# Both MLPs' second layers by seven block products for eight, in passes over K with partial sums in SBUF

## The chip, the cores and the metric

The kernel runs on one core of one Trainium2 chip. The metric is the device time of one execution in microseconds (us). In the views TensorE is PE (its weight loads PEld), VectorE DVE, ScalarE ACT, GpSimd POOL, and SyncE SP, which issues the transfers.

## The reference

Attention with a causal mask over 2 batches, 12 heads, 448 positions and a head width of 64; then two MLPs one after the other on 896 x 768 values, all float32.

```python
def _moe_ref(x, w_gate, w_val, w_out, rms_g):          # 896 x 768, d_ff 1536
    rms = np.sqrt(np.mean(x * x, axis=-1, keepdims=True) + 1e-06)
    xn = x / rms * rms_g
    g = xn @ w_gate
    silu = g * (1.0 / (1.0 + np.exp(-g)))
    val = xn @ w_val
    return (silu * val @ w_out).astype(np.float32)

def _moe2_ref(x, w_in, w_out):                         # d_ff 2048
    h = np.maximum(x @ w_in, 0.0)
    return (h * h @ w_out).astype(np.float32)
```

## The kernel before

Activations lie with the feature along the 128 partitions and the 448 positions of one batch along the free axis; such a tile is called a row here. A layer's output tile is 128 features x 448 positions of one batch, summed over K in tiles of 128.

A float32 product is made of three products in a rounded type (fp32r): each operand is split into a high part (a rounding copy) and a low part (the difference). `parts` splits a row into a slab of high and low part: a cast at line 208 or 210, a subtraction at line 499. `form` does it for three weight tiles into a `ring` buffer: the cast at the same helper's lines, the subtraction at line 608. `product` (line 615) issues the three matmuls of each K tile, 128 x 128 by 128 x 448, into a PSUM bank `m`, at line 623. `weights` loads 128 x 768 of a weight as raw numbers and puts their bits together in two ScalarE steps (lines 571 and 576) and one VectorE step (line 581).

The first layers of both MLPs run through `halves` (line 669): two output tiles and both batches at once, as a 2 x 2 block product over a K of two halves, by seven block products p1 to p7 for eight. It needs sums of weight tiles (`minus`, line 636), four sums of row blocks (`differences`, line 643; the subtraction is at line 652), and adds of PSUM banks and of copies of them (`snap`, line 251 or 694). One such pair is 63 matmuls, where eight block products would be 72. The bank x carries p1, p6, p7 and p4 one on top of the other; after p1, p6 and p7 its running value is taken out before the next product goes on top. The products are issued in the order p1, p2, p6, p5, p7, p4, p3.

The second layers (`layer`, line 857) run directly: for each output tile and both batches, 3 matmuls for each of 12 K tiles (first MLP, w_out as `wo`) or 16 (second MLP, `w2o`, in two passes over K of 10 and 6 tiles; the first pass leaves its sum in a row, the second adds its bank to it at line 940 and stores the output).

Nothing waits in the program's own order. Every step is a task with a due time, the engines that may do it with an estimated duration each, its predecessors and its buffers. `Order.run` takes them one after the other: for each open task the engine is chosen on which it ends first, with COST added for VectorE ("D") and GpSimd ("P"); of the tasks that can start within 0.1 us of the first, that with the earliest due time goes next. GpSimd's steps and those of VectorE marked `port` (inputs in SBUF alone) are planned as excluding each other, one at a time. The result is a fixed order of instructions on each engine. Buffers of a kind are used in turn: a new one waits until the oldest is free. The 24 slabs are two such rings, `sa` (6) and `sb` (18), the rows `fa` (14) and `fb` (18); `sb` and `fb` are there when attention's buffers have been given back.

```python
            first = min(opt, key=lambda c: (c[1], c[2], c[3]))
            c = min((c for c in opt if c[4] == first[4] and c[1] <= first[1] + SLACK), key=lambda c: (c[2], c[3]))
```

## Time and profile before

| | |
|---|---|
| median of 3 runs | 584.4 us (583.57 to 663.83) |
| profiled execution, its own time | 582.35 us |
| its span (first to last instruction) | 580.6 us |
| TensorE busy | 559.5 us (96%), 3155 instructions |
| VectorE, ScalarE, GpSimd busy | 424.4 (73%), 340.9 (59%), 130.4 us (22%) |
| granted TensorE clock, mean | 0.996 |
| HBM read and written | 61.74 and 2.75 MB |

The busy share of an engine is a mean over stages that differ; it is to be read by stage. A wait is put down to the engine and line that released it. A matmul's own duration in the trace overlaps its neighbours', so the pace of TensorE is read from the starts of groups. An operation that may be done by several engines is listed once for each.

### The profile page before, as it was taken

Reading aid. Unit: us, or ns where it says so; the run is one execution under the profiler, and the core shown is the slowest. Engines: PE = TensorE matmul, PEld = TensorE weight load, DVE = VectorE, ACT = ScalarE, POOL = GpSimd, SP = SyncE. Lnnn points to the kernel's source line nnn. Section 1 sums busy time; section 2 is a strip of 40 time slices with the busy share of each in tenths; the row PEclk is TensorE's granted clock in tenths of the full one; section 3 lists DMA queues with packets and bytes.
Section 4 is the critical chain, followed back from the end, with each engine's and each line's share of the span. In section 5 each row is a group of like instructions: output and inputs, shape, how many; then the busy total and the mean of one; then the engine's idle time right before and its main releaser. Section 6 shows DMA issues by size and latency. Waiting matters only on the chain.

```text
span 580.6 us, 8705 instructions
## 1 busy us (share of the span) xinstructions
PE 559.5 (96%) x3155; PEld 495.1 (85%) x3155; DVE 424.4 (73%) x760; ACT 340.9 (59%) x718; POOL 130.4 (22%) x193
## 2 busy tenths in 40 slices
PE   7998998969999999999999999999999999999997
PEld 4766666859899999998999998899999999999996
DVE  4788898768999988998743549999989974336311
ACT  4778887536757676578644446665666665556100
POOL 3555866140022000040000013311213720000000
PEclk9999999989999999999999999999999999999999
DMA  6265421201325333363354211134332345341111
GB/s 174 82 204 151 150 66 77 109 1 58 104 93 183 110 108 110 108 207 119 110 175 145 105 66 56 56 122 144 115 109 91 123 148 179 114 155 64 64 65 63
DMA packets 19499, 65.06 MB, mean 112 GB/s; under 512 B 2048, under 2 KB 8960, under 8 KB 19456
## 3 DMA queue, kind: packets, MB, share of 16 engines
q1 hardware_dynamic: 19456, 64.50, 33.4%
q8 instruction: 25, 0.41, 0.3%
q14 instruction: 18, 0.15, 0.1%
HBM read 61.74 MB, written 2.75 MB: 111 GB/s over the span
## 4 chain that ended last, share of the span: by engine, by line
PE 87%; DVE 7%; POOL 2%; DMA 1%; ACT 1%; issue 1%; SPq 0%; POOLq 0%; DVEq 0%; ACTq 0%
PE m L623 73%; PE t L408 3%; PE o L446 3%; PE s L305 3%; POOL p L392 2%; DVE sb L499 2%; PE s L318 2%; PE s L817 1%; PE o L441 1%; DMA raw<-in_wg 1%; DVE mx L341 1%; DVE fa L548 1%; DMA qk<-in_qk 1%; DVE ring L608 1%; DVE fa L652 0%
## 5 line engine op out<-in xcount | busy, mean ns | idle before, releaser
L623 PE MATMUL m<-sb,ring 128*128 128x448 f32 x1584 | 333.4, 367 | 7.2 <-DVE fa L761 4.9
L623 PEld LDWEIGHTS m<-sb,ring 128*128 128x128 f32 x1584 | 298.4, 189 | 32.3 <-issue 5.2
L623 PE MATMUL m<-sa,ring 128*128 128x448 f32 x630 | 138.1, 365 | 0.9 <-DVE ring L608 0.9
L623 PEld LDWEIGHTS m<-sa,ring 128*128 128x128 f32 x630 | 118.3, 188 | 10.5 <-DVE ring L608 1.3
L210 ACT CAST ring<-w 128x384 fp32r<-128x384 f32 (+1 forms) x111 | 49.6, 471 | 70.0 <-PE m L623 47.4
L608 DVE TENSOR_TENSOR ring<-w,ring 128x384 fp32r<-128x384 f32 (+1 forms) x111 | 57.6, 537 | 40.8 <-ACT ring L210 40.6
L576 ACT ACTIVATE raw<-raw 128x768 uint32<-128x768 uint8 x70 | 62.4, 894 | 12.1 <-DMA raw<-in_wv 8.6
L581 DVE SCALAR_TENSOR_TENSOR w<-w,raw 128x768 uint32<-128x768 uint32 x64 | 53.1, 831 | 20.9 <-ACT w L571 11.2
L208 POOL TENSOR_SCALAR ring<-st 128x384 fp32r<-128x384 f32 x23 | 12.1, 530 | 222.4 <-DVE st L636 124.4
L571 ACT ACTIVATE w<-raw 128x768 f32<-128x768 f32 x64 | 53.6, 850 | 12.7 <-DVE ring L608 9.3
L608 DVE TENSOR_TENSOR ring<-st,ring 128x384 fp32r<-128x384 f32 x65 | 35.7, 573 | 9.0 <-POOL ring L208 5.6
L210 ACT CAST ring<-st 128x384 fp32r<-128x384 f32 x49 | 24.7, 514 | 18.5 <-DVE st L636 14.7
L341 DVE TENSOR_REDUCE mx<-s 128x2 f32<-128x256 f32 (+2 forms) x36 | 24.0, 686 | 12.3 <-PE s L321 6.7
L251 ACT COPY snap<-m 128x448 f32<-128x448 f32 x37 | 19.8, 534 | 19.6 <-PE m L623 19.3
L392 POOL TENSOR_SCALAR p<-p,r 128x128 f32<-128x128 f32 (+1 forms) x48 | 24.0, 518 | 24.9 <-DVE r L382 18.4
L305 PE MATMUL s<-qk 64*128 64x128 f32 (+2 forms) x144 | 26.5, 448 | 2.3 <-ACT p L366 1.1
L392 POOL TENSOR_SCALAR p2t<-p2t,r 128x256 f32<-128x256 f32 (+1 forms) x36 | 21.9, 625 | 11.0 <-DVE r L382 8.4
L366 ACT ACTIVATE p<-s,nb 128x128 f32<-128x128 f32 (+1 forms) x48 | 22.1, 473 | 1.3 <-ACT nb L346 0.4
L446 PE MATMUL o<-pt,vt 128*64 128x320 f32 (+2 forms) x192 | 20.2, 353 | 0.0
L408 PE MATMUL t<-ident,p 128*128 128x128 f32 x96 | 14.2, 283 | 5.8 <-POOL p L392 5.0
L251 ACT COPY fb<-m 128x448 f32<-128x448 f32 x21 | 11.1, 535 | 14.8 <-PE m L623 14.3
L499 DVE TENSOR_TENSOR sb<-fb,sb 128x448 fp32r<-128x448 f32 x29 | 19.6, 710 | 0.0
(125 smaller groups left out, 623.3 us busy)
## 6 DMA issues: line engine op xcount, KB each, us to landing
raw<-in_w2i SPq DMA_DIRECT2D x16, 768.0 KB, 4.2
raw<-in_wg SPq DMA_DIRECT2D x12, 768.0 KB, 4.7
raw<-in_wv SPq DMA_DIRECT2D x12, 768.0 KB, 4.3
raw<-in_wo SPq DMA_DIRECT2D x12, 768.0 KB, 4.6
raw<-in_w2o SPq DMA_DIRECT2D x12, 768.0 KB, 4.4
qk<-in_qk SPq DMA_DIRECT2D x11, 448.0 KB, 3.8
raw<-in_w2o SPq DMA_DIRECT2D x6, 512.0 KB, 3.9
vt<-in_v SPq DMA_DIRECT2D x12, 128.0 KB, 2.8
```

Source lines behind the costliest of these rows:

```text
L210: eng.copy(o, i)
L251: (nc.scalar.copy if e == "A" else nc.vector.tensor_copy)(o, i)
L305: nc.tensor.matmul(s[:, h, o:o + n], z["qk"][BOTH[h], 0, qs], z["qk"][BOTH[h], 1, :n], start=True, stop=False)
L392: E(e).tensor_scalar(t, t, z["r"][:, k:k + 1], 1.0, ALU.mult, ALU.mult)
L408: nc.tensor.transpose(t[:, i * P:(i + 1) * P], src[:, o * P:(o + 1) * P], ident)
L446: nc.tensor.matmul(z["o"][BOTH[h], S - n:S], z["v"][:, j, h * D:(h + 1) * D], z["pt"][:, h, KO[j]:KO[j] + n], start=j == 0, stop=j == 3)
L499: E(e).tensor_sub(bs.tile[:, 1], bf.tile, bs.tile[:, 0].bitcast(F32))
L571: nc.scalar.activation(bt.tile[:, :n * P], br.tile[:, :n * P, 1].bitcast(F32), AF.Prelu, scale=2.0 ** -112, alpha=2.0 ** 32)
L576: nc.scalar.activation(br.tile[:, :n * P, 0], b, AF.Copy, scale=1.0 / 32, bias=-31.0 / 64)
L581: nc.vector.scalar_tensor_tensor(dst.tile.bitcast(U32) if dst else u, u, 3, br.tile[:, a:b, 0], ALU.logical_shift_left, ALU.bitwise_or)
L608: E(e).tensor_sub(br.tile[:, 1, :n], num(), br.tile[:, 0, :n].bitcast(F32))
L623: nc.tensor.matmul(bank.tile[:, :S], bw.tile[:, a, i], x[:, c], start=first and i == 0 and k == 0, stop=last and i == n - 1 and k == 2, sk ...
```

## The change

Both second layers run through `halves` as well, six K tiles at a time, which is what its block form takes. The first MLP's `wo`: K tiles 0 to 5 by sevens (three pairs of output tiles), then 6 to 11 directly (`whole`, which calls `layer` for one chunk) on top. The second MLP's `w2o`: K tiles 0 to 3 directly, then 4 to 9 and 10 to 15 by sevens. Between passes the sums of the 12 output tiles (6 for each batch) lie in rows. Where such a sum exists already, `halves` gets it as `sums`: the running values of bank x are added into it on VectorE (line 707 of the changed kernel) where they were copied, and the rest is added by `kept` (line 909). Each pass by sevens has its own 9 splits and 12 differences with their 12 splits (`halved`).

Buffers are no longer taken in turn: each kind has places, and a task takes the one that was free first. The slabs are one kind (`part`, 6 + 18) and the rows one (`row`, 14 + 18); there are five `snap` for four. COST becomes 0.4 for both VectorE and GpSimd.

```diff
-COST = {"D": 0.3, "P": 0.6}
+COST = {"D": 0.4, "P": 0.4}
...
+    def free(self, pool):
+        p = [x for x in self.places.get(pool, ()) if x[0] is None or not x[0].left]
+        return sorted(p, key=lambda x: x[0].end + 0.2 if x[0] else 0.0)
...
     def ready(self, t):
...
+            p = self.free(b.pool)
+            if len(p) < k:
+                return None
+            if p[k - 1][0]:
+                s = max(s, p[k - 1][0].end + 0.2)
...
-    caps = dict(raw=2, wt=2, st=5, ring=8, snap=4, tt=2, uu=2, sa=6, sb=18, fa=14, fb=18, m=4, w=2)
...
+    have(pw, raw=2, wt=2, st=5, ring=8)
+    have(pt_, snap=5, tt=2, uu=2, part=6, row=14)
...
+        have(p, part=18, row=18)
...
+        have(ctx.enter_context(tc.tile_pool(name="ps_m", bufs=1, space=PSUM)), m=4, w=2)
...
-    def halves(a, b, f, due, done, scale=1.0, begin=0.0, home="w"):
+    def halves(a, b, f, due, done, scale=1.0, begin=0.0, home="w", sums=None):
...
-        def snap(bank, t, due):
-            b = buf("snap")
+        def snap(bank, t, due, i, j):
+            b = sums[j][i][0] if sums else buf("snap")
 
             def g(e):
-                if scale == 1.0:
+                if sums:
+                    nc.vector.tensor_add(b.tile, bank.tile[:, :S], b.tile)
+                elif scale == 1.0:
                     copy(e, b.tile, bank.tile[:, :S])
...
+            if sums:
+                return b, add(due, {"D": D_(S)}, g, [t, sums[j][i][1]], uses=[bank, b])
...
-        layer(wo[dt], hx, 0, [6, 6], due, done)
...
+    def halved(x, k0, prev=()):
+        x = [y[k0:k0 + NCC] for y in x]
+        f = dict(B11=[parts(x[0][j], due - 6 + j, prev) for j in range(3)],
+                 B21=[parts(x[0][j + 3], due - 5 + j, prev) for j in range(3)])
+        f.update(differences(x, due - 4, prev))
+        f.update(B22=[parts(x[1][j + 3], due + j + 6, prev) for j in range(3)])
+        return f
...
+    def kept(sums, i, j, bank, snap, after, due, store=None):
+        old = sums[j][i]
+        bf = old[0] if old else buf("row")
+        def f(e):
+            if snap or old:
+                nc.vector.tensor_add(bf.tile, bank.tile[:, :S], snap.tile if snap else bf.tile)
+            else:
+                copy(e, bf.tile, bank.tile[:, :S])
...
+    def seven(src, k0, f, sums, due, last=False):
+        for a in range(NCC // 2):
+            c = (a, a + NCC // 2)
+            own = [[sums[j][c[i]] for i in range(2)] for j in range(B)]
...
+            halves(src[c[0]][:, k0:k0 + NCC], src[c[1]][:, k0:k0 + NCC], f, due, done,
+                   sums=own if own[0][0] else None)
+            due += 12.8
+        return due
+
+    def whole(src, k0, n, x, sums, due):
+        for a in range(NCC):
+            c = a // 2 + a % 2 * NCC // 2
+            layer(src[c], x, k0, [n], due, lambda b, bank, t, due, c=c: kept(sums, c, b, bank, None, [t], due))
...
+    g = halved(hf, 0, highs(f))
+    due = seven(wo, 0, g, yf, due)
+    hx = split(hf, NCC, NCC, highs(g))
+    due = whole(wo, NCC, NCC, hx, yf, due)
+    f = halved(yf, 0, highs(hx))
...
-    K1 = 10
...
-            layer(w2o[dt], hx, k0, chunks, due, done)
...
+    hx = split(h2, 0, 4, highs(f))
+    due = whole(w2o, 0, 4, hx, of, due)
+    f = halved(h2, 4, highs(hx))
+    due = seven(w2o, 4, f, of, due)
+    g = halved(h2, 10, highs(f))
+    due = seven(w2o, 10, g, of, due, True)
```

What this does to the order on the engines is shown at three places. TensorE in the last layer (the program's end; `m` are banks, `sa`, `sb` and `part` slabs, `ring` weights). Before, one output tile over the last six K tiles, each weight for both batches:

```order
L623 MATMUL m_5666<-sb_4931,ring_5517 128x448 x3
L623 MATMUL m_5666<-sb_4946,ring_5517 128x448 x3
L623 MATMUL m_5666<-sb_5393,ring_5517 128x448 x3
L623 MATMUL m_5678<-sb_4944,ring_5517 128x448 x3
L623 MATMUL m_5678<-sb_4949,ring_5517 128x448 x3
L623 MATMUL m_5678<-sb_5408,ring_5517 128x448 x3
L623 MATMUL m_5666<-sb_5410,ring_5541 128x448 x3
L623 MATMUL m_5666<-sa_5419,ring_5541 128x448 x3
L623 MATMUL m_5666<-sa_5434,ring_5541 128x448 x3
L623 MATMUL m_5678<-sa_5414,ring_5541 128x448 x3
L623 MATMUL m_5678<-sa_5422,ring_5541 128x448 x3
L623 MATMUL m_5678<-sa_5448,ring_5541 128x448 x3
```

In the changed kernel, in the last pass by sevens (K tiles 10 to 15), p6, p5 and p7 of the first pair and p1 of the second:

```order
L639 MATMUL m_5700<-part_5600,ring_5672 128x448 x3
L639 MATMUL m_5700<-part_5640,ring_5672 128x448 x3
L639 MATMUL m_5700<-part_5645,ring_5672 128x448 x3
L639 MATMUL m_5809<-part_5680,ring_5676 128x448 x3
L639 MATMUL m_5809<-part_5712,ring_5676 128x448 x3
L639 MATMUL m_5809<-part_5717,ring_5676 128x448 x3
L639 MATMUL m_5700<-part_5715,ring_5694 128x448 x3
L639 MATMUL m_5700<-part_5720,ring_5694 128x448 x3
L639 MATMUL m_5700<-part_5724,ring_5694 128x448 x3
L639 MATMUL m_5846<-part_5392,ring_5759 128x448 x3
L639 MATMUL m_5846<-part_5398,ring_5759 128x448 x3
L639 MATMUL m_5846<-part_5592,ring_5759 128x448 x3
```

The bank m_5700 is written by p6, read, and written by p7 with one product on another bank (m_5809) between; each product reads three slabs of its own. VectorE near the end of the last layer: `w` are weights in PSUM, `st` weight sums in SBUF, `fa` and `row` the rows of the output. Before:

```order
L608 TENSOR_TENSOR ring_5517<-w_5466,ring_5517 128x384
L940 TENSOR_TENSOR fa_4982<-m_5479,fa_4982 128x448
L940 TENSOR_TENSOR fa_4996<-m_5495,fa_4996 128x448
L608 TENSOR_TENSOR ring_5541<-w_5466,ring_5541 128x384
L608 TENSOR_TENSOR ring_5565<-w_5505,ring_5565 128x384
L940 TENSOR_TENSOR fa_5088<-m_5531,fa_5088 128x448
L940 TENSOR_TENSOR fa_5101<-m_5546,fa_5101 128x448
L608 TENSOR_TENSOR ring_5589<-w_5505,ring_5589 128x384
```

And in the changed kernel, for the products just shown (the running value after p6 is taken by the add into row_5093, that after p7 by the add into row_5151):

```order
L909 TENSOR_TENSOR row_5351<-m_5662,row_5351 128x448
L651 TENSOR_TENSOR st_5803<-st_5763,w_5740 128x384
L651 TENSOR_TENSOR st_5806<-st_5803,w_5697 128x384
L707 TENSOR_TENSOR row_5093<-m_5700,row_5093 128x448
L651 TENSOR_TENSOR st_5823<-w_5697,st_5763 128x384
L624 TENSOR_TENSOR ring_5821<-st_5806,ring_5821 128x384
L624 TENSOR_TENSOR ring_5825<-st_5803,ring_5825 128x384
L651 TENSOR_TENSOR st_5841<-w_5697,st_5806 128x384
L624 TENSOR_TENSOR ring_5837<-st_5823,ring_5837 128x384
L707 TENSOR_TENSOR row_5151<-m_5700,row_5151 128x448
L909 TENSOR_TENSOR row_5151<-m_5809,row_5151 128x448
L624 TENSOR_TENSOR ring_5857<-w_5740,ring_5857 128x384
```

Between products there were weight steps and two adds for an output tile; now there are sums of weights, their low parts and an add for nearly every product. GpSimd in attention, about two thirds through it: `p1` and `p2t` are probabilities scaled by `r`, `ring` weight parts, `snap` a sum of squares, `rs` a reciprocal root. Before:

```order
L392 TENSOR_SCALAR p1_855<-p1_855,r_829 128x128 x2
L392 TENSOR_SCALAR p1_855<-p1_855,r_829 128x384 x2
L392 TENSOR_SCALAR p2t1_129<-p2t1_129,r_829 128x256 x2
L392 TENSOR_SCALAR p2t1_129<-p2t1_129,r_829 128x448
L522 TENSOR_TENSOR rs_997<-rin_965,mhalf_89 112x4
L392 TENSOR_SCALAR p1_968<-p1_968,r_938 128x128 x2
L392 TENSOR_SCALAR p1_968<-p1_968,r_938 128x384 x2
L608 TENSOR_TENSOR ring_1012<-wt_897,ring_1012 128x384
L392 TENSOR_SCALAR p2t0_127<-p2t0_127,r_938 128x256 x2
L392 TENSOR_SCALAR p2t0_127<-p2t0_127,r_938 128x448
L392 TENSOR_SCALAR p1_1083<-p1_1083,r_1045 128x128 x2
L392 TENSOR_SCALAR p1_1083<-p1_1083,r_1045 128x384 x2
```

And in the changed kernel:

```order
L624 TENSOR_TENSOR ring_893<-wt_781,ring_893 128x384
L416 TENSOR_SCALAR p1_853<-p1_853,r_823 128x128 x2
L416 TENSOR_SCALAR p1_853<-p1_853,r_823 128x384 x2
L539 TENSOR_TENSOR rs_950<-rin_942,mhalf_89 112x4
L232 TENSOR_SCALAR ring_983<-wt_781 128x384
L416 TENSOR_SCALAR p2t1_129<-p2t1_129,r_823 128x256 x2
L416 TENSOR_SCALAR p2t1_129<-p2t1_129,r_823 128x448
L416 TENSOR_SCALAR p1_960<-p1_960,r_929 128x128 x2
L416 TENSOR_SCALAR p1_960<-p1_960,r_929 128x384 x2
L624 TENSOR_TENSOR ring_992<-wt_841,ring_992 128x384
L624 TENSOR_TENSOR ring_1001<-wt_841,ring_1001 128x384
L416 TENSOR_SCALAR p2t0_127<-p2t0_127,r_929 128x256 x2
```

More low parts of weights stand between the scalings.

## Rows read from the trace of the kernel before

**Rows 1.** The page: busy time by engine; the last chain by line.

```profile
PE 559.5 (96%) x3155; PEld 495.1 (85%) x3155; DVE 424.4 (73%) x760; ACT 340.9 (59%) x718; POOL 130.4 (22%) x193
PE m L623 73%; PE t L408 3%; PE o L446 3%; PE s L305 3%; POOL p L392 2%; DVE sb L499 2%; PE s L318 2%; PE s L817 1%; PE o L441 1%; DMA raw<-in_wg 1%; DVE mx L341 1%; DVE fa L548 1%; DMA qk<-in_qk 1%; DVE ring L608 1%; DVE fa L652 0%
```

**Rows 2.** Stretch, us, busy us (count) of PE, PEld, DVE, ACT, POOL; clock, DMA.

```profile
0.00:122.00 122.00, 108.06 (x941) 78.42 (x941) 96.37 (x198) 87.08 (x260) 63.49 (x116) 1.00 0.38 121
122.00:266.00 144.00, 141.85 (x690) 130.76 (x691) 127.70 (x232) 92.36 (x168) 24.73 (x31) 0.99 0.33 110
266.00:354.00 88.00, 88.00 (x436) 81.57 (x435) 49.32 (x81) 48.34 (x84) 5.30 (x6) 1.00 0.34 117
354.00:458.00 104.00, 102.48 (x504) 94.31 (x504) 98.75 (x169) 63.61 (x118) 26.60 (x30) 1.00 0.31 103
458.00:577.00 119.00, 119.00 (x588) 110.05 (x586) 51.65 (x84) 49.55 (x90) 10.28 (x11) 1.00 0.32 110
```

**Rows 3.** TensorE's timeline, 275 to 302 us: start, us, line, operation, count.

```profile
275.79 22.05 PE L623 MATMUL m<-sb,ring 128*128 128x448 f32 x108
297.67 3.81 PE L623 MATMUL m<-sa,ring 128*128 128x448 f32 x18
```

**Rows 4.** Waits of TensorE from 122 us on: us in total, times, longest.

```profile
PE m L623 <- DVE fa L761: 4.9, 1, 4.9
PE m L623 <- ACT snap L694: 1.7, 2, 1.1
PE m L623 <- DVE ring L608: 0.9, 1, 0.9
PE m L623 <- DVE snap L251: 0.6, 1, 0.6
```

**Rows 5.** VectorE by line and shape: busy us, mean ns of one.

```profile
L581 DVE SCALAR_TENSOR_TENSOR w<-w,raw 128x768 uint32<-128x768 uint32 x41 | 39.3, 962 | 18.7 <-ACT w L571 10.5 <-ACT raw L576 8.2
L581 DVE SCALAR_TENSOR_TENSOR w<-w,raw 128x384 uint32<-128x384 uint32 x17 | 9.6, 566 | 0.5
L608 DVE TENSOR_TENSOR ring<-w,ring 128x384 fp32r<-128x384 f32 x105 | 56.0, 551 | 39.4 <-ACT ring L210 39.2
L608 DVE TENSOR_TENSOR ring<-st,ring 128x384 fp32r<-128x384 f32 x65 | 35.7, 573 | 9.0 <-POOL ring L208 5.6 <-ACT ring L210 3.1
L636 DVE TENSOR_TENSOR st<-st,w 128x384 f32<-128x384 f32 x34 | 18.7, 550 | 0.6
L940 DVE TENSOR_TENSOR fb<-m,fb 128x448 f32<-128x448 f32 x6 | 3.7, 625 | 18.1 <-PE m L623 18.1
L906 DVE SCALAR_TENSOR_TENSOR fb<-fb 128x448 f32<-128x448 f32 x18 | 14.1, 782 | 0.5
```

**Rows 6.** The same view: low parts of splits, differences, copies of banks.

```profile
L499 DVE TENSOR_TENSOR sb<-fb,sb 128x448 fp32r<-128x448 f32 x29 | 19.6, 710 | 0.0
L499 POOL TENSOR_TENSOR sb<-fb,sb 128x448 fp32r<-128x448 f32 x9 | 11.7, 1300 | 5.8 <-ACT sb L210 5.3
L499 POOL TENSOR_TENSOR sb<-fa,sb 128x448 fp32r<-128x448 f32 x5 | 5.8, 1160 | 20.4 <-ACT sb L210 19.3 <-DVE sb L499 1.1
L652 DVE TENSOR_TENSOR fb<-fa,fb 128x448 f32<-128x448 f32 x4 | 2.5, 618 | 0.0
L251 ACT COPY snap<-m 128x448 f32<-128x448 f32 x37 | 19.8, 534 | 19.6 <-PE m L623 19.3
```

**Rows 7.** Timeline of all engines around 358 us.

```profile
...
356.86 1.48 POOL L652 TENSOR_TENSOR fa<-fb 128x448 f32<-128x448 f32 x1 [5.20 <-ACT fb L251]
...
357.24 1.58 DVE L652 TENSOR_TENSOR fa<-fb,fa 128x448 f32<-128x448 f32 x1
358.74 0.55 DVE L608 TENSOR_TENSOR ring<-w,ring 128x384 fp32r<-128x384 f32 x1
...
359.34 0.87 PE L623 MATMUL m<-sa,ring 128*128 128x448 f32 x3 [0.90 <-DVE ring L608]
```

**Rows 8.** Waits of TensorE up to 123 us.

```profile
PE t L408 <- POOL p L392: 5.0, 8, 1.5
```

More of the change, by code (lines that the diff above doesn't have):

```diff
@@ L278, in step @@
         bq, bv, b1, b2, bp1, bp2 = (order.buf(n) for n in ("qk", "v", "s", "s", "p1", "p2"))
[L279 removed]
+        bpt, bo, bx = (order.buf(n) for n in ("pt", "o", "row"))
         def load_qk(e):
@@ L827, in rows_come @@
         p = ctx.enter_context(tc.tile_pool(name="later", bufs=1))
-        have(p, "sb", "fb")
-    late["sb"] = late["fb"] = add(0.0, {"X": 0.0}, rows_come, used)
+        have(p, part=18, row=18)
+    add(0.0, {"X": 0.0}, rows_come, used)
     norm(0, (NPAIR + 3.5) * STRIDE, 8.0)
@@ L842, in banks_come @@
         attps.close()
-        have(ctx.enter_context(tc.tile_pool(name="ps_m", bufs=1, space=PSUM)), "m", "w")
-    late["m"] = add(0.0, {"X": 0.0}, banks_come, used_ps + [x[1] for b in xs for x in b])
+        have(ctx.enter_context(tc.tile_pool(name="ps_m", bufs=1, space=PSUM)), m=4, w=2)
+    add(0.0, {"X": 0.0}, banks_come, used_ps + [x[1] for b in xs for x in b])
     whole_tiles(1, ws, 1010.0)
@@ L873, in layer @@
             k += n
-    hx = [[None] * NF1, [None] * NF1]
-    for i in range(NF1):
-        for b in range(B):
-            hx[b][i] = parts(hf[b][i], due - 5 + i, [x[1] for y in f.values() for x in y])
-    yf = [[], []]
-    for dt in range(NCC):
-        def done(b, bank, t, due):
-            bf = row()
-            def f(e):
-                copy(e, bf.tile, bank.tile[:, :S])
-            yf[b].append((bf, add(due, c2opt(S), f, [t], new=[bf], uses=[bank], prev=[late[bf.pool]])))
-        layer(wo[dt], hx, 0, [6, 6], due, done)
-        due += 14.6
@@ new lines, in highs, with g @@
+    def highs(f):
+        return [x[1] for y in (f.values() if isinstance(f, dict) else f) for x in y]
+    def kept(sums, i, j, bank, snap, after, due, store=None):
[4 more added lines that the diff above has]
+                nc.vector.tensor_add(bf.tile, bank.tile[:, :S], snap.tile if snap else bf.tile)
+            else:
+                copy(e, bf.tile, bank.tile[:, :S])
+        t = add(due, {"D": D_(S)} if snap or old else c2opt(S), f, list(after) + ([old[1]] if old else []),
+                new=[] if old else [bf], uses=[bank] + ([bf] if old else []) + ([snap] if snap and not old else []))
+        sums[j][i] = (bf, t)
+        if store is not None:
+            def g(e):
+                nc.sync.dma_start(out=out[store * P:(store + 1) * P, j * S:(j + 1) * S], in_=bf.tile)
+            add(due, {"S": 2.0}, g, [t], uses=[bf])
+        return t
@@ L908, in squared @@
         if snap:
-            r = add(due, {"D": D_(S)}, whole, after, new=[bf], uses=[bank, snap], prev=[late[bf.pool]])
+            r = add(due, {"D": D_(S)}, total, after, new=[bf], uses=[bank, snap])
         else:
-            r = add(due, c2opt(S), copied, after, new=[bf], uses=[bank], prev=[late[bf.pool]])
+            r = add(due, c2opt(S), copied, after, new=[bf], uses=[bank])
         t = add(due, {"D": D_(S)}, square, [r], uses=[bf])
```

139 lines of the change are left out of this document (60 added, 79 removed).

## The prediction

> **What bounds the kernel now.** I read the page's engine shares and chain first [rows 1]: TensorE is busy 96% of the span, and its products of line 623 alone make 73% of the chain that ended last; no other engine's line has a comparable share. The table by stages [rows 2] says where this holds: attention to 122 us, the first MLP's first layer to 266, its second layer to 354, the second MLP's first layer to 458, its second layer to 577. TensorE is busy all of both second layers (88.00 of 88.00 us, 119.00 of 119.00), at a granted clock of 1.00, while VectorE is busy for 49.32 and 51.65 us of them. In the two first layers, which already run seven block products for eight, VectorE is busy 127.70 of 144 and 98.75 of 104 us, and yet all that TensorE waits for after 122 us is 8.1 us, 4.9 of them at the hand-over from attention [rows 4]. So the stages to be changed are the ones that TensorE bounds with much room beside it, and the stage from 354 to 458 us shows what the same form costs when it is full.
>
> **The gain.** 108 products start at 275.79 and the next follow at 297.67 us [rows 3]: 21.88 / 108 = 0.2026 us each, with no gap. Both second layers hold 432 + 576 = 1008 products, 204.2 us. After the change: w_out of the first MLP 3 pairs x 63 + 216 direct = 405; of the second 144 direct + 6 x 63 = 522. 81 fewer, **16.4 us** off TensorE if it stays fed.
>
> **What is added on VectorE, per pair of output tiles.** A pair with sums in SBUF: the bits of two weight tiles 0.962 + 2 x 0.566, seven low parts of weights, three from PSUM and four from SBUF (3 x 0.551 + 4 x 0.573), four weight sums (0.550 each), and seven adds at the price of the add of line 940 (0.62): 2.09 + 3.95 + 2.20 + 4.37 = 12.6 us [rows 5]. The pair takes TensorE 63 x 0.2026 = 12.8 us. A pair of the stage 354 to 458 costs three such adds and four squares (0.782) instead of the seven adds: 2.09 + 3.95 + 2.20 + 1.87 + 3.13 = 13.2 us. That is more than the new pair, and it ran at TensorE's pace [rows 2, 4], because some low parts went to GpSimd. The first MLP's pairs have no sums to add to: three adds, 10.1 us. So the pairs themselves are covered.
>
> Each halved pass also needs 21 splits and 12 differences, where 12 splits stood. In the whole kernel that is 128 splits for 101, and 60 differences for 24. In the order, VectorE does 58 low parts of splits (82 before) and 26 differences (16); GpSimd does 70 (19) and 34 (8). For the second MLP's last layer, VectorE gets 6 x 12.6, six direct tiles at no more than 0.962 + 2 x 0.551 each, 14 low parts at 0.71 and 8 differences at 0.62 [rows 5, 6]: 75.6 + 12.4 + 9.9 + 5.0 = 103 us at most, in 522 x 0.2026 = 105.8 us of TensorE. It goes from less than half full to as full as the stage 354 to 458 was (95%). ScalarE gets 38 casts more, each of the size of its copies at 0.534 us [rows 6], in stages where it stood at 42 to 64% [rows 2]: nothing. The weight loads are as many and as large as before, and the DMA share is about a third [rows 2]: nothing.
>
> **Waits on partial sums.** In a pass with sums the bank's running value is taken by an add on VectorE, where ScalarE mostly copied (0.534 us, [rows 6]). Three of seven products of a pair go on in a bank that was just read. The order leaves one product, 1.8 us, between p6 and p7 and one between p7 and p4, three before p6, so an add of 0.62 us that starts within 1.2 us costs nothing. Cover gone, each costs what it is late. Only the last pair has p7 and p4 back to back; the old order has that once too (at the end of the first MLP's first layer, inside the 1.7 us of [rows 4]): nothing net.
>
> **Buffers.** Slabs of split rows are 24 as before. Counted from the order at 0.2026 us a product, a slab now comes free 12.2 us or more before its next content is used, but for one at 9.7 (the second MLP's entry); before it was 10.9 or more, and that ran. Nothing, with 0 to 1 us for the one.
>
> **The shared SBUF access.** At 356.86 us GpSimd starts a difference (1.48 us), at 357.24 VectorE starts another, which takes 1.58 instead of 0.62; the weight part behind it is late, and TensorE waits 0.90 us for it [rows 6, 7]. With the 0.6 us behind VectorE's copy that follows [rows 4], an entry into a halved stage cost 1.5 us, from some 33 two-input GpSimd operations after attention. These become 119 (all together 131 for 39). In proportion that is 5.4 us, 3.9 more; the least is nothing, since the planner never sets the two side by side on purpose. I take **2.5 us**, nearer to the proportion, because the sevens of the last layer leave VectorE no room. The Trainium skill states this as a rule (SBUF — State Buffer, section "Who interferes with whom"): a VectorE instruction with two SBUF inputs and a GpSimd instruction that reads SBUF exclude each other, and the second waits until the first is through. The trace agrees, roughly: of the 1.48 us 1.10 were left, plus 0.62 is 1.72, where 1.58 were taken. By the row alone I add 2.5 us; by the rule at every chance meeting the time would be that of the first rival, 576.6.
>
> **Attention.** The two costs set equal move squares, sums and weight parts to GpSimd: 12 two-input operations for 6 up to its last scaling of probabilities, at 1.2 to 1.5 us [rows 6, 7], in the queue ahead of the scalings for which TensorE's transposes waited 5.0 us already [rows 8]. All six more in the way would cost 7 us or over. Against that VectorE loses seven such operations at 0.65 (4.5 us), at 79% busy, and the new order puts transposes a block later. Bounds -2 to +4; I take **+1.0**.
>
> **Sum.** -16.4 + 2.5 + 1.0 = -12.9 us. The profiled execution took 582.35 us with a span of 580.6; that becomes 569.5 and 567.7. The median of the runs shown is 584.4, 2.0 above: 571.5 us.
>
> **Rivals.**
> *The shared access takes the room.* In the last layer GpSimd holds about 40 two-input operations at 1.2 us, 45% of its 105.8 us; VectorE has 46 of its own that need the same access (14 low parts, 8 differences, 24 low parts of weights from SBUF). Met by chance, each waits half of 1.2 us with chance 0.45: 12.4 us on top of 103, so 115 in 105.8, of which I count 2 us for the upper bounds taken there: TensorE 7.6 us late. Gain 16.4 - 7.6 - 1.0 = 7.8: 576.6 us. For it: [rows 7] and the shares. Against: in the stage 354 to 458 GpSimd was busy 26.60 us beside a full VectorE, at a cost of 1.5 us.
> *All is covered.* The new entry into the second MLP needs 12 splits beforehand instead of 24, so VectorE reaches it with more in hand, and the 1.5 us vanish as well: 16.4 + 1.5 = 17.9, 566.5 us. Against: [rows 7] shows a collision that no plan intended.
> *Adds too late, and slower than before.* 18 adds (three in each of six pairs with sums) stand between two products of a bank. VectorE works in order, so an add behind one weight operation (0.962) still fits its 1.8 us, behind two it doesn't. From a mean lateness of 12.9 / 18 = 0.72 us on, the gain is gone; at 1.0 us it is 18, or 589.5 us. It would take two operations in front of nearly each; the order shows one or two of 0.55 there.
>
> **Chances.** The forecast case, 568.5 to 575 us, 0.58; the shared access, 575 to 580, 0.22; all covered 0.13; late adds 0.07. About 2% (11.7 us, 572.7 us) is what a measurement of this kernel can tell from no change. Two thirds of the first case lie below that line: 0.38 + 0.13 = 0.51 faster. Slower by over 2% needs adds 1.4 us late each, half of the last case: 0.03. The rest 0.46. The range from 567 to 579 us leaves out half of the covered case, the upper edge of the second and the last, 0.17 together.
>
> **What would show it.** Right: 2133 products at 0.2026 us; TensorE's waits after attention 4 to 6 us without the hand-over's, at entries and behind VectorE; VectorE busy near 95% in the last layer, GpSimd some 240 us over all; first product of line 639 within 2 us of 122.5. Wrong: a wait that recurs in each of the last six pairs behind the adds of lines 707 and 909 (late adds), VectorE's low parts at over 1 us in the mean (shared access), or a first product of line 639 after 125 us (attention).

## The result, and the profile after

| | before | after |
|---|---|---|
| median, runs of the comparison | 585.23 us | 576.19 us (576.02 to 577.52, 4 runs) |
| ratio of the two | | 0.986, 95% interval 0.983 to 0.989 |
| profiled execution, its own time | 582.35 us | 576.15 us |
| TensorE's products | 2214 | 2133 |

Faster by 1.4%, less than the 2% that was set as the bound: the class that had 0.46. The time lies in the range (567 to 579) and 4.7 us above the 571.5 forecast. 16.4 us of products went; the profiled execution shows 6.2 of them. The ratio leaves out the one execution of the kernel before that took 663.83 us, which its median contains.

The last chain by engine in the page of the kernel before, and engines and last chain in that of the changed one, to be held against [rows 1]:

```profile
PE 87%; DVE 7%; POOL 2%; DMA 1%; ACT 1%; issue 1%; SPq 0%; POOLq 0%; DVEq 0%; ACTq 0%
```

```profile
PE 551.5 (96%) x3074; PEld 483.0 (84%) x3074; DVE 487.9 (85%) x853; ACT 359.7 (63%) x757; POOL 250.6 (44%) x301
...
PE 62%; DVE 24%; ACT 4%; issue 4%; DMA 3%; POOL 2%; SPq 0%; DVEq 0%; ACTq 0%; POOLq 0%
```

VectorE now holds 24% of the last chain where it held 7%: something in it ends last, and more often. The table by stages (columns as in [rows 2]; second layers 266 to 352 and 460 to 571 us) shows where TensorE is no longer always busy:

```profile
0.00:122.00 122.00, 111.10 (x941) 80.49 (x941) 93.16 (x192) 86.49 (x259) 67.81 (x123) 0.99 0.39 121
...
266.00:352.00 86.00, 84.49 (x418) 77.97 (x417) 70.71 (x119) 56.32 (x102) 27.01 (x25) 1.00 0.40 126
352.00:460.00 108.00, 106.69 (x522) 97.44 (x521) 102.21 (x171) 67.83 (x129) 49.95 (x49) 1.00 0.31 100
460.00:571.00 111.00, 106.78 (x511) 96.51 (x509) 93.09 (x157) 56.43 (x103) 46.31 (x44) 0.98 0.34 112
```

Both second layers were free of gaps in [rows 2]; now 1.5 and 4.2 us are missing there, the last at a granted clock of 0.98. TensorE's waits from 122 us on:

```profile
PE m L639 <- DVE row L773: 5.1, 1, 5.1
PE m L639 <- ACT snap L275: 2.8, 3, 1.5
PE m L639 <- ACT row L275: 2.6, 1, 2.6
PE m L639 <- DVE row L707: 0.8, 1, 0.8
PE m L639 <- ACT snap L711: 0.8, 2, 0.4
PE m L639 <- DVE row L959: 0.7, 1, 0.7
```

The first is the hand-over, as in [rows 4]. The others make 7.7 us against 3.2 before. The largest two lines are ScalarE's copies of banks, an operation that costs 0.53 us and that I had put at nothing. The places, in the timelines of TensorE and ScalarE (start, us; idle time before in brackets), at 283, 367 and 488 us:

```profile
283.35 2.90 PE L639 MATMUL m<-part,ring 128*128 128x448 f32 x13 [1.51 <-ACT snap L275]
...
282.33 0.97 ACT L275 COPY snap<-m 128x448 f32<-128x448 f32 x2
...
366.75 1.92 PE L639 MATMUL m<-part,ring 128*128 128x448 f32 x8 [1.06 <-ACT snap L275]
...
365.74 0.97 ACT L275 COPY snap<-m 128x448 f32<-128x448 f32 x2
...
485.73 0.86 ACT L588 ACTIVATE w<-raw 128x768 f32<-128x768 f32 x1 [0.69 <-DVE ring L624]
486.52 1.01 ACT L234 CAST part<-row 128x448 fp32r<-128x448 f32 x2
487.45 0.52 ACT L275 COPY row<-m 128x448 f32<-128x448 f32 x1
...
488.02 3.49 PE L639 MATMUL m<-part,ring 128*128 128x448 f32 x10 [2.63 <-ACT row L275]
```

At 283 and at 367 us two copies stand one behind the other, and TensorE goes on when the second is done. At 488 us TensorE's last product ended at 485.39, and the copy stands behind an exponent and two casts. What follows the 2.63 us is a second loss. The stretches around it, with the granted clock in the third column from the right:

```profile
480.00:488.00 8.00, 5.39 (x27) 4.66 (x25) 6.04 (x12) 5.22 (x9) 3.89 (x5) 1.00 0.52 183
488.00:492.00 4.00, 3.98 (x12) 3.59 (x13) 3.93 (x7) 1.87 (x3) 3.07 (x4) 0.60 0.65 203
```

For 3.4 us the granted clock stood at 0.5, its lower level (1.2 GHz): eight products started 0.373 us behind the one before instead of 0.2027, and with the two at the edges of the stretch (0.32 and 0.28 us) that is 1.6 us.

**A balance that can be made for each profile.** From the starts of the products of `product`: the first one; their number at 0.2027 us; starts at the lower clock (0.33 to 0.38 us apart, less one product); gaps (other starts more than 0.23 us apart, less one product); and what the rest take above 0.2027 us ("pace", below). Behind the last start 3.8 us are left (4.2 in e4).

| profile | own time | first product | products | gaps | lower clock | pace |
|---|---|---|---|---|---|---|
| before | 582.35 | 122.46 | 448.7 | 4.6 | 1.2 | 0.0 |
| after | 576.15 | 122.72 | 432.3 | 10.9 | 3.1 | 1.8 |
| e1, costs as before | 586.05 | 125.58 | 432.3 | 16.5 | 4.1 | 2.2 |
| e2, w_out alone | 577.14 | 120.80 | 443.2 | 5.3 | 2.4 | 0.0 |
| e3, w2o alone | 575.53 | 120.46 | 437.8 | 8.7 | 2.2 | 1.0 |
| e4, no sevens | 586.86 | 120.22 | 448.7 | 2.0 | 1.9 | 8.3 |
| e5, copies in any order | 567.57 | 122.16 | 432.3 | 6.0 | 1.7 | 0.1 |
| e6, two more rows | 569.87 | 120.18 | 432.3 | 8.9 | 2.1 | 1.0 |
| e7, both | 568.64 | 120.71 | 432.3 | 7.2 | 1.9 | 1.2 |
| e8, low parts on VectorE | 580.58 | 121.98 | 432.3 | 14.9 | 1.9 | 4.2 |
| e9, costs alone | 586.32 | 121.01 | 448.7 | 4.0 | 2.4 | 4.5 |
| e10, order mended | 566.59 | 121.48 | 432.3 | 6.4 | 1.0 | 0.0 |
| e11, last bank | 568.52 | 120.97 | 432.3 | 4.7 | 2.4 | 2.8 |
| e12, squares counted | 567.05 | 120.66 | 432.3 | 2.9 | 2.1 | 3.8 |

So of the 16.4 us, 6.3 went into gaps, 1.9 into the lower clock and 1.8 into the pace. The lower clock's 1.9 are 1.4 behind the stop at 488 us and 0.5 at the hand-over, where every profile has it, for 6 to 14 products (1.0 to 2.4 us); a small difference in that column says little about an edit.

**How the products are read for the pace.** The rows of line 639 by source give a count, the shortest, middle and longest duration, and the first and last start: of the changed kernel from 290 to 360 and from 531 to 565 us, and of e4 from 380 to 480 us:

```profile
L639 PE MATMUL m<-part,ring x347: 362/365/369, 289.7 to 359.9; 128*128 128x448 f32 x174
...
L639 PE MATMUL m<-part,ring x167: 368/368/368, 530.7 to 565.0; 128*128 128x448 f32 x167
```

```profile
L639 PE MATMUL m<-part,ring x485: 367/368/369, 379.8 to 479.8; 128*128 128x448 f32 x162
```

70.2 / 346 = 0.203 us from start to start, 34.3 / 166 = 0.207 and 100.0 / 484 = 0.207. All three stretches have no wait in them.

### The profile page after: what moved, and what is told of

Its sections match the earlier page's. It is cut to its first block, busy times and chain, and to the rows that moved or that the text cites. A ratio compares the mean times of both kernels' runs of the same rounds, so it can differ in the third digit from the quotient of the medians.

```text
span 574.4 us, 8858 instructions
## 1 busy us (share of the span) xinstructions
PE 551.5 (96%) x3074; PEld 483.0 (84%) x3074; DVE 487.9 (85%) x853; ACT 359.7 (63%) x757; POOL 250.6 (44%) x301
## 4 chain that ended last, share of the span: by engine, by line
PE 62%; DVE 24%; ACT 4%; issue 4%; DMA 3%; POOL 2%; SPq 0%; DVEq 0%; ACTq 0%; POOLq 0%
PE m L639 50%; DVE ring L624 5%; DVE part L516 4%; PE t L432 3%; PE s L329 3%; PE o L470 3%; DVE w L598 2%; DVE st L651 2%; PE s L342 2%; DVE row L667 2%; DVE row L965 2%; DVE row L959 1%; DMA raw<-in_w2i 1%; DMA raw<-in_wv 1%; POOL p L416 1%
## 5 line engine op out<-in xcount | busy, mean ns | idle before, releaser
L639 PE MATMUL m<-part,ring 128*128 128x448 f32 x2133 | 440.4, 368 | 12.8 <-DVE row L773 5.1
L639 PEld LDWEIGHTS m<-part,ring 128*128 128x128 f32 x2133 | 402.6, 189 | 50.7 <-issue 6.6
L516 POOL TENSOR_TENSOR part<-row,part 128x448 fp32r<-128x448 f32 x70 | 89.4, 1297 | 65.5 <-ACT part L234 65.0
L593 ACT ACTIVATE raw<-raw 128x768 uint32<-128x768 uint8 (+1 forms) x70 | 62.8, 897 | 16.2 <-DMA raw<-in_wv 7.4
L234 ACT CAST ring<-w 128x384 fp32r<-128x384 f32 x102 | 46.8, 468 | 34.1 <-PE m L639 19.5
L588 ACT ACTIVATE w<-raw 128x768 f32<-128x768 f32 (+1 forms) x64 | 54.6, 853 | 13.4 <-DVE ring L624 7.8
L667 POOL TENSOR_TENSOR row<-row 128x448 f32<-128x448 f32 x34 | 45.4, 1353 | 40.0 <-DVE row L965 16.7
L234 ACT CAST part<-row 128x448 fp32r<-128x448 f32 x95 | 51.0, 568 | 15.0 <-DVE row L909 7.3
L624 DVE TENSOR_TENSOR ring<-w,ring 128x384 fp32r<-128x384 f32 x102 | 53.2, 532 | 6.4 <-ACT ring L234 6.1
L598 DVE SCALAR_TENSOR_TENSOR w<-w,raw 128x768 uint32<-128x768 uint32 (+1 forms) x64 | 49.3, 770 | 2.3 <-ACT w L588 1.7
L516 DVE TENSOR_TENSOR part<-row,part 128x448 fp32r<-128x448 f32 x58 | 43.8, 777 | 2.7 <-ACT part L234 2.3
```

The source lines that it names most:

```text
L234: eng.copy(o, i)
L516: E(e).tensor_sub(bs.tile[:, 1], bf.tile, bs.tile[:, 0].bitcast(F32))
L588: nc.scalar.activation(bt.tile[:, :n * P], br.tile[:, :n * P, 1].bitcast(F32), AF.Prelu, scale=2.0 ** -112, alpha=2.0 ** 32)
L593: nc.scalar.activation(br.tile[:, :n * P, 0], b, AF.Copy, scale=1.0 / 32, bias=-31.0 / 64)
L598: nc.vector.scalar_tensor_tensor(dst.tile.bitcast(U32) if dst else u, u, 3, br.tile[:, a:b, 0], ALU.logical_shift_left, ALU.bitwise_or)
L624: E(e).tensor_sub(br.tile[:, 1, :n], num(), br.tile[:, 0, :n].bitcast(F32))
```

## The experiments

Theory A is the prediction's: what TensorE loses comes from the shared SBUF access and grows with GpSimd's two-input operations. Theory B: each new entry into a pass costs a wait, whoever does the work. Theory C: the planner's costs act through attention. Theory O, below, came out of the first four runs. Ratios are against the kernel before, timed beside.

**Which part of the change costs what (e1 to e4).** e1 sets the costs back; e2 and e3 give one of the second layers its old form, e4 both.

```diff
e1:
-COST = {"D": 0.4, "P": 0.4}
+COST = {"D": 0.3, "P": 0.6}
e2 and e4 (w2o direct, passes of 10 and 6 tiles):
-    hx = split(h2, 0, 4, highs(f))
-    due = whole(w2o, 0, 4, hx, of, due)
-    f = halved(h2, 4, highs(hx))
-    due = seven(w2o, 4, f, of, due)
...
+    hx = split(h2, 0, 10, highs(f))
+    for dt in range(NCC):
+        layer(w2o[dt], hx, 0, [6, 4], due, lambda b, bank, t, due, c=dt: kept(of, c, b, bank, None, [t], due))
...
e3 and e4 (wo direct):
-    g = halved(hf, 0, highs(f))
-    due = seven(wo, 0, g, yf, due)
...
+    hx = split(hf, 0, NF1, highs(f))
+    for dt in range(NCC):
+        layer(wo[dt], hx, 0, [6, 6], due, lambda b, bank, t, due, c=dt: kept(yf, c, b, bank, None, [t], due))
```

> All of the change except that the planner's two costs go back to 0.3 for VectorE and 0.6 for GpSimd. GpSimd then does 109 operations with two SBUF inputs after attention, where the changed kernel does 124 and the kernel before about 33. Theory A (what TensorE loses comes from the shared SBUF access, so it grows with the number of those operations): TensorE's waits after the hand-over fall from 7.7 us to about 6.5, time 574 to 576 us. Theory B (each new entry into a pass costs a wait because the first weights and splits of a pass queue up in front of the copies that free banks, whoever does them): the waits stay at 7 to 8 us, 575.5 to 577 us. Theory C (the equal costs are what hurts, or what helped, attention): the first product of line 639 moves from 122.7 us by more than 1 us, and the time with it.

> Only the first MLP's second layer runs by sevens; the second MLP's second layer runs directly as before (passes of 10 and 6 tiles). 27 products fewer than before, 5.5 us at 0.2026 us. Theory A (shared access): 86 two-input operations of GpSimd after attention against about 33, so a loss of some 4 to 5 us: the gain nearly vanishes, ratio 0.997 to 1.002. Theory B (a wait at each new entry, here the ones near 283 and 367 us, 1.5 and 1.1 us, and nothing in the last layer): loss about 2 us, ratio 0.992 to 0.996.

> Only the second MLP's second layer runs by sevens; the first MLP's runs directly as before. 54 products fewer than before, 10.9 us at 0.2026 us. Theory A (shared access): 96 two-input operations of GpSimd after attention against about 33, a loss of 5 to 6 us: ratio 0.990 to 0.993. Theory B (a wait at each new entry, here the ones near 465 and 488 us, 0.7 and 2.6 us, the slow clock behind the second): loss about 4 to 5 us if the long wait comes again, ratio 0.988 to 0.991; 1 to 2 us if it does not, ratio 0.983 to 0.985.

> Both second layers run directly as before; only the equal costs of the planner and the buffers taken where one is free stay of the change. Products as before. If the equal costs and the buffers do nothing by themselves (my prediction, plus 1 us in attention): ratio 0.999 to 1.003. Theory A (shared access): 58 two-input operations of GpSimd after attention against about 33, 1 to 2 us more of waits. If a good part of the missing gain of the full change comes from here, the ratio is 1.005 or more.

| | median | ratio, 95% interval |
|---|---|---|
| e1 | 584.24 us | 0.997 (0.993 to 1.001) |
| e2 | 577.33 us | 0.989 (0.982 to 0.995) |
| e3 | 575.15 us | 0.982 (0.977 to 0.987) |
| e4 | 582.44 us | 0.996 (0.993 to 1.000) |

Theory A misses the sign twice. Counted in the traces from 122 us on, e1 has fewer two-input operations on GpSimd than the changed kernel (105 for 117) and more gaps (16.5 us for 10.9); e4 has more than before (51 for 32) and fewer gaps (2.0 for 4.6). (The 109, 124 and 58 of the expectations hold attention's too, the 33 does not.) e1 also says what the equal costs are worth together with the sevens: without them the 81 products fewer gain nothing, and its median is 8.1 us above the changed kernel's, outside theory B's forecast too. Of the 9.9 us between the two profiles 5.6 are gaps and 2.9 a later first product. For theory C that lateness proves little: e1's profile has two stretches in attention, at 13.5 to 16.8 and 92.0 to 95.3 us, at a granted clock of 0.50. Gaps and lower clock together: e4 3.9 us, e2 7.7, e3 10.9, after 14.0. Against e4, w_out by sevens adds 3.8 us, w2o 7.0, both 10.1: the loss goes with the passes, about as much for each (w2o has two), as theory B has it. e2's and e3's medians were better than either theory said, since the rest of the change gains by itself (e4), which I hadn't expected. e4's own profile shows little of it because of the pace, 8.3 us.

**Why a pass costs (e5 to e7).** In the order, the first new pass (w_out) has TensorE do p1 and p2 of the first pair, p6, then p1 and p2 of the second pair, and only then p5 and p7 of the first, since their splits come later. The copy of the second pair's bank could be made as soon as its p1 is done; but `chain` gives each task that takes a new buffer the last one before it in the code as a predecessor (`prev=[self.last.get(b.pool) for b in new]`). So it must go behind the first pair's third copy, and that one waits for p7. This was right for rings, and it stayed when the rings went. It accounts for the two copies in a row at 282.33 and at 365.74 us. The copy at 487.45 us takes a row for a partial sum, and there are 32 places; in the order the copy comes once a low part of a split has given one back. Theory O: the waits are in the order itself, by these two rules.

```diff
e5 and e7:
-            return b, chain(due, {"A": A_(S), **({"D": D_(S)} if scale == 1.0 else {})}, g, [t], new=[b], uses=[bank])
+            return b, add(due, {"A": A_(S), **({"D": D_(S)} if scale == 1.0 else {})}, g, [t], new=[b], uses=[bank])
e6 and e7:
+    def more_rows(e):
+        for i in range(2):
+            order.more("row", lambda i=i: pw.tile([P, S], F32, tag=f"wt{i}", name="row", bufs=1))
+
+    add(0.0, {"X": 0.0}, more_rows, [t for t in order.tasks if any(b.pool == "wt" for b in t["uses"])])
```

> One word changes against the changed kernel: the copies of a running bank into a snap buffer are no longer issued in the order in which the code creates them (that rule was for rings; the buffers are now taken where one is free). Theory O (the waits stand in the order itself: at 283 and 367 us TensorE took up the next pair's products early, its copy of the bank must then go behind the copy that belongs to the pair before, and that one waits for its product): both waits, 1.5 and 1.1 us, vanish, about 2.6 us, 572.5 to 574.5 us. Theory A (shared SBUF access: the two low parts of 1.25 and 1.58 us on VectorE just ahead of 278 us make everything behind them late): the collisions are still there and so are the waits, 575.5 to 577 us.

> Two more row buffers (in the room of the two wt tiles once these are no longer used), 34 for 32 behind the first MLP's first pairs; nothing else. Theory O (the 2.63 us at 488 us are a wait for a row buffer: the 12 partial sums of the second MLP's last layer want places while 24 of its 32 input rows still stand in theirs, so the copy that frees the bank waits for a split of a later row): the wait falls under 1 us and the clock does not drop to its lower level behind it (1.6 us), 572 to 574 us. Theory A (shared access) or ScalarE's queue (the copy stands behind an exponent and two casts): more places change neither, 575.5 to 577 us.

> Copies in any order and two more row buffers together. Theory O: all three long waits are gone (1.5, 1.1 and most of 2.6 us) and the clock drop with them, some 6 us less than the changed kernel: 569 to 571.5 us. Theory A: one or none of them goes, 574 us or more.

| | median | ratio, 95% interval |
|---|---|---|
| e5 | 567.56 us | 0.971 (0.966 to 0.976) |
| e6 | 571.50 us | 0.976 (0.971 to 0.981) |
| e7 | 569.05 us | 0.972 (0.967 to 0.978) |

e5's median is 8.6 us below the changed kernel's, for one word. By the balances 4.9 us of that are gaps and 1.4 the lower clock; 1.7 are the pace and 0.6 the first product, which no wait that the word removes accounts for. e6's profile is 6.3 us below the changed kernel's, but 2.5 of them are the first product, ahead of anything that its edit touches; gaps and lower clock make 3.0. TensorE's waits from 122 us on in e5, and in e6:

```profile
PE m L639 <- DVE row L773: 4.9, 1, 4.9
PE m L639 <- ACT row L275: 1.1, 1, 1.1
PE m L639 <- DVE row L707: 1.0, 2, 0.8
PE m L639 <- DVE part L516: 0.9, 1, 0.9
PE m L639 <- ACT snap L711: 0.3, 1, 0.3
```

```profile
PE m L639 <- ACT snap L275: 3.4, 4, 1.5
...
PE m L639 <- ACT row L275: 0.7, 2, 0.4
```

In e5 the waits for copies into `snap` buffers by line 275 are gone (2.8 us in the changed kernel); in e6 they are all there and the wait for the row's copy falls from 2.6 to 0.7 us, with no lower clock behind it. So each rule has the waits that theory O puts down to it, with a correction for the rows (below). e6's median lies 0.5 us below its forecast and e7's inside its own. e5 gained more than was expected of it, because its different order also cut the row's wait to 1.1 us and kept the clock up. For the same reason the two do not add up: e7 has e5's gaps and a little more, at other places.

Two things can be added from the order that the kernel computes. The planner's own times have TensorE idle at these three places, among others (1.62, 1.62 and 2.94 us), with e5's word only at the last (2.41), with e6's two rows at the first two and for 0.81 us at the last: so the waits do stand in the order. As prices these times are rough; for the kernel before they add up to 8.1 us after attention, where [rows 4] has 3.2 behind the hand-over. And the rows are not full for the reason given in e6's expectation, that 24 of the 32 input rows still stand. When TensorE stops, the places hold 12 input rows, 7 partial sums and 13 differences. 11 of these differences belong to the last pass (K tiles 10 to 15); their splits are planned 40 us later or more. Nothing makes a difference wait until its pass is near; only the splits have predecessors (`prev`) that do. In the changed kernel's trace, VectorE makes six of them ahead of the stop:

```profile
473.26 4.37 DVE L667 TENSOR_TENSOR row<-row 128x448 f32<-128x448 f32 x6
```

In the planner's times the wait is gone, without more places, when the differences are given these predecessors too; no run has tried that.

And theory A: VectorE's operations with two SBUF inputs, by line and shape from 122 us on (count, busy us, mean ns), in the changed kernel and in e5:

```profile
L624 DVE TENSOR_TENSOR ring<-st,ring 128x384 fp32r<-128x384 f32 x92 | 62.9, 710 | 6.3 <-ACT ring L234 5.5 <-POOL ring L232 0.6
...
L516 DVE TENSOR_TENSOR part<-row,part 128x448 fp32r<-128x448 f32 x48 | 38.0, 812 | 2.1 <-ACT part L234 2.1
```

```profile
L624 DVE TENSOR_TENSOR ring<-st,ring 128x384 fp32r<-128x384 f32 x91 | 65.0, 742 | 5.4 <-ACT ring L234 5.1
...
L516 DVE TENSOR_TENSOR part<-row,part 128x448 fp32r<-128x448 f32 x49 | 41.1, 852 | 1.9 <-ACT part L234 1.9
```

They are stretched in both, no less in the faster kernel ([rows 5, 6] had 573 and, for the larger group of low parts, 710 ns). Counting all such operations that took over 0.15 us more than the lower quarter of their line and shape (line 598 left out, where one input lies in PSUM): 24 before (14 us in all), 59 after (39 us), 65 in e5 (36 us). The Trainium skill (SBUF — State Buffer, section "Who interferes with whom") says that VectorE operations with two SBUF inputs and GpSimd operations that read SBUF exclude each other. The trace of the changed kernel agrees: each of the 59 ran while GpSimd was busy, of the other 162 such operations 26 did. But e5 shows that little of it reached TensorE. What is left of it there is the 0.9 us behind `part` L516 at 278.7 us, where VectorE's low part took 1.56 us. In the changed kernel one wait more has stretched operations straight ahead of it on VectorE, the 0.7 us behind line 959 at 465 us:

```profile
458.74 2.80 DVE L516 TENSOR_TENSOR part<-row,part 128x448 fp32r<-128x448 f32 x2
```

A third low part (1.12 us) and a square (0.90 us) follow before the add. That the wait comes from them is argued, not tested.

**The other way to fewer meetings (e8).**

```diff
-        return bs, add(due, {"P": P_(S, True), "D": D_(S)}, low, [t], uses=[bf, bs], port=True)
+        return bs, add(due, {"D": D_(S)}, low, [t], uses=[bf, bs], port=True)
```

> The low parts of the splits are made on VectorE alone. After attention GpSimd then has 69 operations with two SBUF inputs instead of 124 (the differences and weight parts stay free to go to either). Theory A (what is lost grows with the shared SBUF access): the 7.7 us of TensorE's waits fall towards 4.5 us, 572 to 575 us. Theory O with VectorE's load (an entry into a halved pass brings some 33 operations of 0.62 us that have to be through within a pair or two, and VectorE cannot take them alone): waits grow by some 10 us, to 17 or 19, 583 to 589 us.

579.88 us, ratio 0.990 (0.987 to 0.993): slower than the changed kernel, with 14.9 us of gaps. TensorE's waits in it that are new or longer:

```profile
PE m L639 <- ACT snap L711: 3.5, 2, 2.5
PE m L639 <- DVE part L516: 2.4, 2, 2.2
```

Fewer two-input operations on GpSimd, and waits behind low parts that the changed kernel has not. Of the 4.4 us between the two profiles gaps make 4.0 and the pace 2.4; lower clock and first product are 1.2 and 0.7 less. The direction is theory O's; the size is below the 583 to 589 us expected.

**The costs alone (e9).** The kernel before with `COST = {"D": 0.4, "P": 0.4}`.

> The kernel before with the planner's two costs set equal (0.4 and 0.4) and nothing else. My prediction put 1.0 us of loss in attention on this edit and some of the 2.5 us of shared access: ratio 1.000 to 1.005, first product of line 623 at 123 us or later. The other reading (the profiles of e2, e3 and e4 have that product at 120.2 to 120.8 us, where before had 122.46): attention gains about 2 us, ratio 0.995 to 0.998. If e4's gain comes from the buffers instead, this run shows none.

583.73 us, ratio 0.997 (0.993 to 1.001). The time doesn't decide; the waits up to 123 us do, in e9 and in the changed kernel:

```profile
PE t L408 <- POOL p L392: 3.2, 5, 1.0
```

```profile
PE t L432 <- POOL p L416: 2.1, 4, 0.9
```

[rows 8] had 5.0 us, and e1, with the old costs, has 5.1 again. So equal costs relieve the transposes. The first product comes at 121.0 us in e9 and between 120.2 and 122.7 in the others with equal costs. The late end of that is a slower start and not the order: the changed kernel's and e6's TensorE carry out the same instructions there, and eight transposes take, in the one and in the other,

```profile
13.77 1.97 PE L432 MATMUL t<-ident,p 128*128 128x128 f32 x8
```

```profile
13.11 1.22 PE L432 MATMUL t<-ident,p 128*128 128x128 f32 x8 [0.50 <-POOL p L416]
```

From 20 us on the changed kernel is 2.4 us behind e6 and stays so to the end of attention. The kernel before started as fast as e6 (the same transposes 1.2 us). So 122.46 us is to be compared with e6's 120.18 or e9's 121.01.

**Mending the order (e10 to e12).** e11 is e5 with the last pair's p4 in the free fourth bank; e10 adds another order of the passes, e12 (on e11) counts the squares among those that need the shared access.

```diff
e10, e11, e12:
+        if tail:
+            q, (bq, tq) = buf("m"), sums[0][1]
+            def early(e):
+                nc.vector.tensor_add(bq.tile, x.tile[:, :S], bq.tile)
+            sums[0][1] = bq, add(due + 9 - SOON, {"D": D_(S)}, early, [p7, tq], uses=[x, bq])
+            p4 = product(q, fa22, f["T4"], due + 14.5, True, True)
+            done(1, 0, q, None, [p4], due + 16.5 - SOON, False)
...
e10:
+    f = halved(h2, 0, highs(f))
+    due = seven(w2o, 0, f, of, due)
+    hx = split(h2, NCC, 4, highs(f))
+    due = whole(w2o, NCC, 4, hx, of, due)
+    g = halved(h2, 10, highs(hx))
e12:
-        t = add(due, {"D": D_(S)}, square, [r], uses=[bf])
+        t = add(due, {"D": D_(S)}, square, [r], uses=[bf], port=True)
```

> The changed kernel with copies in any order, the last layer's passes in the order seven (K tiles 0 to 5), direct (6 to 9), seven (10 to 15), so that 12 input rows are given back before the 12 partial sums have to stand somewhere, and the very last pair's fourth product into the free fourth bank instead of the bank that was just read. Theory O: of the waits of e5 (after the hand-over 3.3 us) the one behind the row buffer (1.1 us) and the one at the end (0.8 us) go: 565 to 567 us. Theory A: nothing in it touches the shared access, 567 to 569 us.

> e5 (copies in any order) with the very last pair's fourth product into the free fourth bank; the passes stay in the changed kernel's order. Theory O: against e5 only the wait of 0.8 us (a gap of 1.18 us) near 557 us goes, 566 to 567.5 us; if the wait comes back behind the add of line 909 that now follows, it is 567.5 us or more.

> e11 with one word more: the planner now also keeps GpSimd's operations apart from the 32 squares of line 965 (SBUF in both inputs), which it had placed without regard to the shared SBUF access. In e5's profile 11 of the 32 squares were slowed, by 3.3 us together, and 11 more operations in the first MLP's layers. Theory A (shared access still costs TensorE a good part of what is left): fewer slowed squares and 1.5 us or more less than e11, 564 to 566 us. Theory O: VectorE's stretched operations in the stage of the squares lie beside TensorE's work (e11 waits under 1.5 us there), so the time stays within 1 us of e11's, apart from what the order happens to do near 481 us, 566 to 568 us.

| | median | ratio, 95% interval |
|---|---|---|
| e10 | 566.89 us | 0.971 (0.970 to 0.973) |
| e11 | 567.86 us | 0.972 (0.970 to 0.975) |
| e12 | 566.46 us | 0.970 (0.963 to 0.977) |

The wait at the end is gone in all three, the row's in e10; e10 has two new ones of 2.5 us together behind copies in the second MLP's first layer. e10 lies in theory O's forecast. e11 lies 0.4 us above its own (567.5 us); the wait that was to go with such a time did not come back, but its profile's pace took 2.8 us. The three can't be told apart in time, but their balances can: e12 has 2.9 us of gaps and 3.8 of pace. Its waits after the hand-over are these two lines, 1.3 us in all:

```profile
PE m L639 <- DVE part L516: 0.7, 1, 0.7
PE m L639 <- ACT row L275: 0.6, 2, 0.3
```

Theory A is not decided by e12 itself: by the count above 10 squares are stretched in it and 13 in e11, hardly fewer (all such operations together 54 and 65). Its median is 1.4 us below e11's, more than theory O's 1 us and less than theory A's 1.5; 566.46 us lies in theory O's range. What its profile gained over e11's is 1.8 us of gaps, about half of it at one place (1.50 us from start to start at 482.6 us in e11, 0.65 at 484.0 in e12). All three beat the kernel before by about 3% and the changed one by about 1.5%.

## Why the prediction was right or wrong

**The gain: right.** 2133 products, and 0.2027 us each wherever the pace is that of [rows 3]; the pace of 0.2067 was not seen in the profile before and took 1.8 us.

**VectorE's work by pairs: right in that it was covered, wrong in place.** Overall the waits behind adds of lines 707, 909 and 959 are 1.5 us. The last layer came to 84% (93.09 of 111), not 95%. GpSimd did not take more operations than the order had (70 low parts and 34 differences, as counted), they took longer (250.6 us, not 240). VectorE's 155 operations that start there add up to 100.9 us of their own durations, near the 103 expected, but one starts some 0.08 us before the one ahead of it has ended, so that they fill 92 us. Adding up mean durations counts that twice, in the 12.6 and 13.2 us of the pairs as well. 95% (102.21 of 108) is the second MLP's first layer again.

**Waits on partial sums: right.** One wait behind line 707, 0.8 us, at the end; the rival of late adds shows nowhere.

**Buffers: the step that failed.** The prediction counted slabs and took them for the buffers; it found 9.7 us of slack or more and put 0 to 1 us. It counted neither the rows, which the 12 partial sums share with input rows and with differences made early, nor the rule that copies are issued in the order of the code, which `chain` kept. These two made the long waits: 1.5, 1.1 and 2.6 us, and behind the last one 1.6 us at the lower clock. e5 took away the first two and more than half of the third, e6 most of the third alone. The view to look at was the order: two copies in a row on ScalarE behind products of two pairs.

**The shared access: wrong as a term.** It was 2.5 us, and the rival that made it 7.6 gave 576.6 us, close to the measured time, for a reason that e1, e4 and e5 speak against. The meetings did come (59 stretched operations for 24), but nearly all lay beside TensorE's work. What reaches TensorE is 0.7 to 0.9 us at one place in e5, e11 and e12, and by argument 0.7 us at 465 us in the changed kernel. The prediction scaled the 1.5 us of one stage by a count of operations; a wait that ends at a copy was not such a cost.

**Attention: wrong in sign.** 1.0 us of loss was put there; the wait for GpSimd's scalings fell from 5.0 to 2.1 us. With an equally fast start the first product came 1.5 to 2.3 us earlier than before (e9, e6). The changed kernel's profile shows none of that (122.72 us for 122.46) because of its slow start, which cost 2.4 us. Over the whole kernel the term was further off: together with the sevens the equal costs are worth 8 us (e1). Which steps behind attention make that was not followed up.

**The sum.** Terms of 2.5 + 1.0 us stood against 10 us that were lost, of which 4.5 are TensorE's waits (7.7 us for 3.2), 1.9 the lower clock, 1.8 the pace, and the rest (1.8) the first products after a wait, each 0.1 us late, and the stops under 0.3 us. That the time still fell into the range of 567 to 579 us is luck in good part: its upper part was there for the shared access, and other losses filled it.

## To carry to other kernels

When a change frees buffers from a fixed turn, look for the other rules that the turn had brought along, here an order among the tasks that take them. Count each kind of buffer over the stretch where old inputs, new sums and early work stand side by side; a planner's own times can already show where the bounding engine will stop. A wait behind a short copy is rarely the copy: ask what stands ahead of it in its engine's order, and why it was put there. And a count of collisions is no cost until a wait of the bounding engine ends at one.

## What the runs showed of the hardware

**Two paces of the same product at the full clock.** Products of 128 x 128 by 128 x 448 in a row start either 0.2027 us apart in the mean (in steps of 0.199 to 0.207 us that repeat) or 0.2067 us apart, each of them. In the balances one or the other holds from one stop of TensorE to the next. In e4, where TensorE stops least, the slower holds from about 150 us on and costs 8.3 us. The granted clock is the same; from 290 to 360 us of the changed kernel (faster pace) and from 380 to 480 us of e4 (slower):

```profile
290.00:360.00 70.00, 70.00 (x347) 64.87 (x346) 53.64 (x92) 43.42 (x75) 18.91 (x19) 1.00 0.38 123
```

```profile
380.00:480.00 100.00, 100.00 (x485) 90.83 (x484) 88.01 (x150) 62.35 (x114) 31.20 (x36) 1.00 0.36 116
```

It is not VectorE's load either: in e4 it goes on through the last layer, where VectorE is busy for 33 of 100 us (480 to 580 us). What chooses it was not found. It is as large as the spread of one kernel's times (e4: 579.89 to 587.97 us in ten runs), but only one execution of each has a trace, so that it makes this spread is not shown.

**The lower clock after a stop.** 2.63 us of waiting at 488 us were followed by 3.4 us at the lower level, and so were waits of 2.4 and 2.0 us in e1; in e3 a wait of 2.3 us at the same copy and in e8 waits of 2.5 and 2.2 us were not. Before the change no wait but the hand-over's was so long.
